# A sparse attention and mixer kernel: the identity made on GpSimd, and the first values and second pair's loads issued without a gate

## The chip, the core and the metric

The kernel runs on one core of a Trainium2 chip. Its time is the device time of one execution in microseconds; the times shown are of four runs, and the profile is of one more execution. The engines are TensorE (PE, with its weight loads as PEld), VectorE (DVE), ScalarE (ACT), GpSimd (POOL) and SyncE (SP), which issues most of the DMAs.

## The reference

The inputs are `q`, `k` and `v` of 4 batches x 8 heads x 768 positions x 64, three sampled blocks of keys for each of 24 blocks of 32 positions, and the weights of a mixer. The attention is masked by blocks: a block of queries sees its own block and its two neighbours, the first and the last block, and its sampled blocks; the first and last blocks of queries see all. The mixer mixes the positions by a low-rank product and then runs a two-layer network over the channels.

```python
scores = (q @ k.T) / sqrt(64);  scores = where(mask, scores, -1e9)
attn = softmax(scores);  x = attn @ v            # heads side by side: (4, 768, 512)
u = x + (x.transpose(0, 2, 1) @ U @ V).transpose(0, 2, 1)
out = u + relu(u @ w_ch1) @ w_ch2                # 512 -> 2048 -> 512
```

## The kernel before

The 32 heads are worked through in 16 pairs, numbered `i`; pairs 0 to 3 (`HP` = 4) make up the first batch. The loads of a pair's `q`, `k` and `v` are 384 KB each, in f32 (`src_of`, `new_ld`, `issue`, L220 to L234), into pools with two buffers of each kind. GpSimd casts them to f16 (`cast`, L236), TensorE transposes queries and keys in blocks of 128x128 by a matmul with an identity matrix `id16` (`turn_some`, L265; the transposed blocks are the tile `pturn`), and VectorE or ScalarE copies them from PSUM to `qa` and `ka` (`half_copy`, L417). The other half of the partitions of `qa` and `ka` holds the mask: `ka` one-hot rows of the key's block, which DMAs bring (`hot_rows`, L299), and `qa` a bias of 0 or -240 for each block of keys, made by a small matmul and a scaling (`mask_mm`, `mask_rows`, L375 to L398). One matmul so gives scores with their mask.

A pair has nine units `u`. For each one, TensorE writes 128x1024 scores (`psc`, L489), ScalarE takes the exponential (`est`, L498, always on ScalarE), and TensorE multiplies with the values three units later (`flush_value`, `pav`). At set units other work is put in by `at_unit` (L984): at unit 0 of pair 0 the second halves of the first queries and keys, the copies of the mask rows to the second set of `qa` (L999, by DMA on SyncE), the load of pair 2's queries and of the mixer's weights (L1003 to L1011), and the casts of pair 1 (L1012 to L1014); at units 4 and 6 the transposes of pair 1's queries and keys.

The order of work on each engine is the order of the program text (`keep`), so an engine that waits holds up all that is written behind it. After the first four pairs (from about 46 us) a planner in the kernel (`clk`, `later`, `try_unit`) lays out the remaining attention units between the matmuls of the mixer's network, in an order that is fixed when the kernel is built.

The start is written out by hand (L287 to L431). VectorE clears `zeros`, the mask halves and other tiles. GpSimd clears `Ut` and `Vt` and writes the column of ones in `vts`. SyncE issues the sampled blocks, the first pair's queries in two pieces (4 and 2 of 6 position groups), the second piece of its keys, and one-hot rows for one head; ScalarE issues a small table of constants, the first piece of the keys, the identity (L313) and one-hot rows for the other head, and then loads its table of exponentials with a dummy activation (L317). TensorE runs six warm-up matmuls on `zeros` (`warm_pe`). GpSimd casts the first piece of the keys, and VectorE that of the queries.

Behind these, the value load of pair 0 has a gate. GpSimd copies one column of the first keys' buffer `kld` into the value buffer `vld` (L335) once the first keys have landed and been cast. The load of `vld` on SyncE (L336) overwrites that column and so waits for the copy, and the three loads of pair 1 (`issue(1)`, L337) stand behind it on SyncE:

```python
vld = new_ld(0, "v")
keep(nc.gpsimd.tensor_copy(out=vld[:, 0, 0, 0:1], in_=kld[:, 0, 0, 0:1]))
keep(nc.sync.dma_start(out=vld, in_=src_of("v", 0)))
issue(1)
```

Of the kernel before, what the change touches and what calls it, by code (L numbers as in the profile page):

```python
# [15 lines left out]
ALU = mybir.AluOpType  # L16

P = 128
# [3 lines left out]
def kernel(  # L22
# [12 lines left out]
    nc = tc.nc  # L35
# [31 lines left out]
        [oh_np[:NB], ms_np, np.tile(np.arange(NB, dtype=np.float16), (NB, 1))], axis=1  # L67
    )
    small_np = np.concatenate([small_np, np.zeros_like(small_np[: 32 - NB])])
    eye16_np = np.eye(P, dtype=np.float16)  # L70

    small_dr = nc.inline_tensor(small_np, name="small_const")
    oh_dr = nc.inline_tensor(oh_np, name="onehot_const")
    eye16_dr = nc.inline_tensor(eye16_np, name="eye16_const")

    consts = ctx.enter_context(tc.tile_pool(name="consts", bufs=1))
    wpool = ctx.enter_context(tc.tile_pool(name="wpool", bufs=1))
# [21 lines left out]
    keep = tc.keep_in_program_order  # L99
# [95 lines left out]
    id16 = consts.tile([P, P], FP16)  # L195
# [7 lines left out]
    zeros = m01[:, T - 1, 0:P]  # L203
# [16 lines left out]
    def src_of(nm, i):  # L220
        b, hp = divmod(i, HP)
        return {"q": q, "k": k, "v": v}[nm][b, 2 * hp : 2 * hp + 2].rearrange(
            "h (p t) d -> p h t d", t=T
        )

    def new_ld(i, nm):
        lds[i, nm] = ldpool.tile([P, 2, T, D], FP32, tag="ld" + nm, name=nm + "ld")
        return lds[i, nm]

    def issue(i, names="qkv"):  # L230
        if i >= NPAIR:
            return
        for nm in names:
            keep(nc.sync.dma_start(out=new_ld(i, nm), in_=src_of(nm, i)))  # L234
# [55 lines left out]
    keep(nc.vector.memset(cbd, 0.0))  # L290
    for r in (slice(32, 64), rows[1]):
        keep(nc.vector.memset(small[r, 0:S], 0.0))
    keep(nc.gpsimd.memset(Ut, 0.0))
    keep(nc.gpsimd.memset(Vt, 0.0))
    qld, kld = new_ld(0, "q"), new_ld(0, "k")
# [3 lines left out]
    def hot_rows(eng, st, h, n):  # L299
# [5 lines left out]
            out=sbi[0:NB].rearrange("z r w -> z (r w)"),  # L305
            in_=sampled_blocks.bitcast(I32),
# [3 lines left out]
    keep(nc.scalar.dma_start(out=small[0:32], in_=small_dr.ap()))  # L310
    keep(nc.scalar.dma_start(out=kld[:, :, 0:TK], in_=k0[:, :, 0:TK]))
    keep(nc.sync.dma_start(out=qld[:, :, TQ:T], in_=q0[:, :, TQ:T]))
    keep(nc.scalar.dma_start(out=id16, in_=eye16_dr.ap()))  # L313
    keep(nc.sync.dma_start(out=kld[:, :, TK:T], in_=k0[:, :, TK:T]))
    hot_rows(nc.scalar, 0, 0, NB)
    hot_rows(nc.sync, 0, 1, NB)
# [6 lines left out]
    def cast0(eng, st, ld, t0, t1):  # L323
        keep(
            eng(
                out=st.rearrange("p t h d -> p h t d")[:, :, t0:t1],
                in_=ld[:, :, t0:t1],
            )
        )

    cast0(nc.gpsimd.tensor_copy, kst, kld, 0, TK)


    vld = new_ld(0, "v")
    keep(nc.gpsimd.tensor_copy(out=vld[:, 0, 0, 0:1], in_=kld[:, 0, 0, 0:1]))  # L335
    keep(nc.sync.dma_start(out=vld, in_=src_of("v", 0)))  # L336
    issue(1)  # L337

    warm = pst_tile([P, 512], FP32, "warm", tag="pav")
# [1 line left out]
    def warm_pe(n):  # L341
        for _ in range(n):
# [9 lines left out]
            out=eq[0:NB],  # L352
# [7 lines left out]
            out=cb[0:NB],  # L360
            in_=eq[0:NB].rearrange("z r c -> z c r"),
# [6 lines left out]
            out=cbd[0:NB, :, 0:NB],  # L368
# [697 lines left out]
    fill = deque()  # L1066
# [195 lines left out]
```

## Time and profile before

| What | Value |
|---|---|
| Four runs, median (lowest to highest) | 280.11 us (279.38 to 281.87) |
| The profiled execution | 279.39 us |
| Its span, from the first to the last instruction | 277.6 us |
| Busy: PE, PEld, DVE, ACT, POOL | 270.2, 161.5, 174.9, 177.2, 103.0 us |
| Granted TensorE clock | 1.0 of full speed |
| Mean DMA rate over the span | 114 GB/s |
| First exponential of ScalarE (L498) | 7.43 us |
| Exponentials of the first four pairs end | 45.71 us |
| First transposes (`pturn` from `qst`) | 5.60 us |
| Issue of the identity's DMA (L313), time to landing | 1.76 us, 3.8 us |

The times in the table's last four rows are from the start of the span. 1.8 us of the profiled execution lie outside its span. An idle time in a row stands before its instruction, and the name behind the arrow is what ended it. An engine's row with "xN" merges N instructions that follow one another. Rows marked SPq, ACTq or POOLq are an engine's DMA issues, which do not count as busy.

### The profile page before, as it was taken

Reading aid. Unit: us, or ns where it says so; the run is one execution under the profiler, and the core shown is the slowest. Engines: PE = TensorE matmul, PEld = TensorE weight load, DVE = VectorE, ACT = ScalarE, POOL = GpSimd, SP = SyncE. Lnnn points to the kernel's source line nnn. Section 1 sums busy time; section 2 is a strip of 40 time slices with the busy share of each in tenths; the row PEclk is TensorE's granted clock in tenths of the full one; section 3 lists DMA queues with packets and bytes.
Section 4 is the critical chain, followed back from the end, with each engine's and each line's share of the span. In section 5 each row is a group of like instructions: output and inputs, shape, how many; then the busy total and the mean of one; then the engine's idle time right before and its main releaser. Section 6 shows DMA issues by size and latency. Waiting matters only on the chain.

```text
span 277.6 us, 8037 instructions
## 1 busy us (share of the span) xinstructions
PE 270.2 (97%) x3492; PEld 161.5 (58%) x3492; DVE 174.9 (63%) x285; ACT 177.2 (64%) x198; POOL 103.0 (37%) x137
## 2 busy tenths in 40 slices
PE   7899999999999999999999999999999999999995
PEld 2568775566656564657565565656565655665443
DVE  6767767878887987777756768777777441000112
ACT  4989996787987857694855749584886201654000
POOL 4569549507374835363604536361102020000000
PEclk9999999999999999999999999999999999999999
DMA  5999975999969999996990999995100323000222
GB/s 140 292 302 302 269 181 84 190 180 82 144 46 94 190 124 140 158 99 78 69 104 0 181 93 169 133 95 77 31 2 2 104 79 94 12 1 0 78 76 77
DMA packets 85664, 31.72 MB, mean 114 GB/s; under 512 B 75308, under 2 KB 83228, under 8 KB 85628
## 3 DMA queue, kind: packets, MB, share of 16 engines
q0 software_dynamic: 49824, 10.29, 42.9%
q1 hardware_dynamic: 35304, 20.66, 35.0%
q8 instruction: 27, 0.44, 0.7%
q10 hardware_dynamic: 500, 0.25, 0.3%
q14 instruction: 9, 0.07, 0.1%
HBM read 27.91 MB, written 6.29 MB: 123 GB/s over the span
## 4 chain that ended last, share of the span: by engine, by line
PE 90%; DMA 4%; DVE 2%; POOL 1%; ACT 1%; issue 0%; ACTq 0%; SPq 0%; POOLq 0%; DVEq 0%
PE pch L175 30%; PE pt L175 30%; PE pav L175 13%; PE psc L175 12%; DMA qld<-in_q_dram 3%; PE pa L175 2%; DMA id<-eye_const 1%; PE ph L175 1%; PE pturn L268 1%; ACT est L498 1%; POOL xh L598 0%; PE puT L711 0%; DVE xh L541 0%; DVE xs L589 0%; PE pmk L175 0%
## 5 line engine op out<-in xcount | busy, mean ns | idle before, releaser
L498 ACT ACTIVATE est<-psc 128x1024 f16<-128x1024 f32 x144 | 143.2, 1028 | 45.5 <-PE psc L175 44.2
L175 PE MATMUL pt<-uT,w1t 64*128 64x384 f16 (+1 forms) x896 | 94.4, 324 | 0.0
L175 PE MATMUL pch<-w2t,tT 64*128 64x512 f16 (+3 forms) x688 | 93.6, 372 | 0.1
L519 DVE TENSOR_TENSOR est<-est,m 128x1024 f16<-128x1024 f16 x108 | 78.2, 739 | 18.2 <-ACT est L498 17.0
L175 PEld LDWEIGHTS <-w1t 64*128 64x128 f16 (+1 forms) x896 | 46.0, 95 | 36.2 <-PE pt L175 8.3
L175 PEld LDWEIGHTS <-tT 64*128 64x128 f16 (+1 forms) x688 | 38.2, 95 | 36.9 <-PE pch L175 1.6
L736 ACT ACTIVATE tT<-pt 128x768 f16<-128x768 f32 (+1 forms) x48 | 36.6, 772 | 26.0 <-PE pt L175 26.0
L175 PEld LDWEIGHTS <-est 128*128 128x128 f16 x1152 | 41.5, 97 | 10.9 <-issue 5.0
L175 PE MATMUL pav<-vt,est 128*128 128x65 f16 x1152 | 44.5, 193 | 0.2
L791 DVE TENSOR_TENSOR of<-xf,pch 128x1024 f32<-128x1024 f32 (+3 forms) x16 | 15.2, 950 | 42.7 <-PE pch L175 42.7
L175 PE MATMUL psc<-qT,kT 64*128 64x512 f16 (+1 forms) x288 | 40.6, 323 | 0.3 <-ACT est L498 0.3
L598 POOL CAST xh<-xs 128x768 f16<-128x768 f32 x12 | 10.5, 872 | 80.1 <-DVE xs L589 74.6
L684 POOL CAST uh<-xf 128x768 f16<-128x768 f32 x12 | 13.9, 1162 | 26.1 <-DVE xf L675 14.5
L738 DVE TENSOR_SCALAR tT<-pt 128x768 f16<-128x768 f32 (+1 forms) x20 | 18.3, 917 | 5.9 <-PE pt L175 5.8
L175 PE MATMUL psc<-qa,ka 128*128 128x512 f16 (+1 forms) x96 | 21.7, 326 | 0.2
L175 PEld LDWEIGHTS <-kT 64*128 64x128 f16 x288 | 14.6, 94 | 12.5 <-issue 0.7
L263 POOL DMA_DIRECT2D vt<-in_v_dram x20 | 16.3, 820 | 2.6 <-DMA w2t<-in_moe_w_ch_dram 2.6
L263 POOL DMA_DIRECT2D qst<-in_q_dram x20 | 16.3, 819 | 0.1
L263 POOL DMA_DIRECT2D kst<-in_k_dram x20 | 16.3, 820 | 0.0
L589 DVE TENSOR_TENSOR xs<-pav,rcp 128x768 f32<-128x768 f32 x12 | 11.5, 958 | 1.2
L675 DVE TENSOR_TENSOR xf<-xs,ph 128x768 f32<-128x768 f32 x12 | 11.4, 950 | 1.2 <-PE ph L175 1.2
L175 PEld LDWEIGHTS <-ka 128*128 128x128 f16 (+1 forms) x108 | 8.5, 97 | 3.5 <-issue 1.6
(69 smaller groups left out, 129.4 us busy)
## 6 DMA issues: line engine op xcount, KB each, us to landing
out_dram<-of SPq DMA_DIRECT2D x9, 512.0 KB, 3.3
vld<-in_v_dram SPq DMA_DIRECT2D x6, 384.0 KB, 7.0
w1t<-in_moe_w_ch_dram POOLq DMA_DIRECT2D x4, 512.0 KB, 8.7
w2t<-in_moe_w_ch_dram POOLq DMA_DIRECT2D x4, 512.0 KB, 9.8
qld<-in_q_dram SPq DMA_DIRECT2D x5, 384.0 KB, 6.2
kld<-in_k_dram SPq DMA_DIRECT2D x5, 384.0 KB, 6.7
qst<-in_q_dram POOLq DMA_DIRECT2D x20, 96.0 KB, 4.0
kst<-in_k_dram POOLq DMA_DIRECT2D x20, 96.0 KB, 4.5
```

Of the source, the lines that this page charges most:

```text
L175: ins = nc.tensor.matmul(out, lhsT, rhs, start=start, stop=stop, skip_group_check=loose)
L263: keep(nc.gpsimd.dma_start(out=o[:, h], in_=src_of(nm, i)[:, h]))
L268: nc.tensor.transpose(out=pt[:, t, :], in_=st[:, t].rearrange("p h d -> p (h d)"), identity=id16,)
L498: keep(nc.scalar.activation(out=est, in_=psc, func=AF.Exp, scale=0.125))
L519: keep(nc.vector.tensor_tensor(out=o, in0=o, in1=m, op=ALU.mult))
L589: nc.vector.tensor_tensor(out=xs.rearrange("p (c j) (h d) -> p c (j h) d", c=2, h=2), in0=pv[:, :, :, 0:D], in1=rcp[:, :, :, None].broadca ...
L598: keep(nc.gpsimd.tensor_copy(out=xh, in_=xs))
L675: nc.vector.tensor_tensor(out=u.rearrange("p (c j) n -> p c j n", c=2), in0=xs.rearrange("p (c j) n -> p c j n", c=2), in1=ph[:, :, 0:HS]. ...
L684: keep(nc.gpsimd.tensor_copy(out=uh, in_=u))
L736: keep(nc.scalar.activation(out=o, in_=i, func=AF.Relu))
L738: keep(nc.vector.tensor_scalar_max(out=o, in0=i, scalar1=0.0))
L791: nc.vector.tensor_add(out=of, in0=xfs[b][:, sc : sc + nsc, n0:n1], in1=pch)
```

## The change

The identity is no longer a constant in memory that a DMA on ScalarE's queue brings. GpSimd makes it in SBUF as its first work: an affine select reads `zeros` and writes 1 where the column's number equals the partition's, and the value read (0) elsewhere. GpSimd's column copy is gone, and the value load of pair 0 is issued by the same helper as the others, with nothing between it and SyncE's one-hot rows before it. The rest of the program, and the order on every engine, stays.

```diff
-    eye16_np = np.eye(P, dtype=np.float16)
...
-    eye16_dr = nc.inline_tensor(eye16_np, name="eye16_const")
...
     for r in (slice(32, 64), rows[1]):
         keep(nc.vector.memset(small[r, 0:S], 0.0))
+    keep(
+        nc.gpsimd.affine_select(
+            out=id16, in_=zeros, pattern=[[-1, P]], compare_op=ALU.not_equal,
+            fill=1.0, base=0, channel_multiplier=1,
+        )
+    )
     keep(nc.gpsimd.memset(Ut, 0.0))
...
     keep(nc.sync.dma_start(out=qld[:, :, TQ:T], in_=q0[:, :, TQ:T]))
-    keep(nc.scalar.dma_start(out=id16, in_=eye16_dr.ap()))
     keep(nc.sync.dma_start(out=kld[:, :, TK:T], in_=k0[:, :, TK:T]))
...
     cast0(nc.gpsimd.tensor_copy, kst, kld, 0, TK)
-
-
-    vld = new_ld(0, "v")
-    keep(nc.gpsimd.tensor_copy(out=vld[:, 0, 0, 0:1], in_=kld[:, 0, 0, 0:1]))
-    keep(nc.sync.dma_start(out=vld, in_=src_of("v", 0)))
+    issue(0, "v")
     issue(1)
```

## The prediction

> **What bounds the kernel now.** The page comes first, for the whole; then the busy time by stage, ScalarE's instructions in order of time, the chain of waits up to 25 us, and SyncE's issues. Busy time by stage (us, and instructions of each engine):
>
> ```profile
> 0.00:7.40 7.40, 5.50 (x20) 1.85 (x21) 4.71 (x15) 2.81 (x5) 3.80 (x13) 1.00 0.53 138
> 7.40:45.70 38.30, 36.43 (x521) 26.51 (x521) 27.65 (x61) 37.09 (x39) 25.37 (x39) 1.00 0.91 248
> 45.70:277.60 231.90, 228.24 (x2956) 133.14 (x2952) 142.50 (x211) 137.33 (x155) 73.87 (x87) 1.00 0.78 91
> ```
>
> The columns after the length are PE, PEld, DVE, ACT, POOL, then TensorE's granted clock (1.00), the DMA share and GB/s. From 45.7 us on TensorE is busy 228.24 of 231.90: that stage starts when the one before it ends, and a shift at its start goes through to the end. From 7.4 to 45.7 us ScalarE is the tightest engine, 37.09 of 38.30 us, and its gaps tell which wait ends last (the timeline of ScalarE; start, length, count, and the idle time before):
>
> ```profile
> 7.43 6.90 ACT L498 ACTIVATE est<-psc 128x1024 f16<-128x1024 f32 x7 [0.54 <-PE psc L175]
> 15.15 10.45 ACT L498 ACTIVATE est<-psc 128x1024 f16<-128x1024 f32 x11 [0.83 <-PE psc L175]
> ...
> 23.67 19.88 ACT L498 ACTIVATE est<-psc 128x1024 f16<-128x1024 f32 x21
> 43.77 1.94 ACT L498 ACTIVATE est<-psc 128x1024 f16<-128x1024 f32 x2 [0.22 <-PE psc L175]
> ```
>
> From the first exponential at 7.43 to 45.71 there are two gaps, 0.83 and 0.22 us. What lies behind the large one stands in TensorE's and GpSimd's timelines:
>
> ```profile
> 14.18 0.51 PE L268 MATMUL pturn<-id,kst 128*128 128x128 f16 x6 [0.89 <-POOL kst L249]
> ...
> 5.22 0.40 POOL L325 CAST kst<-kld 128x256 f16<-128x256 f32 x1 [2.61 <-DMA kld<-in_k_dram]
> 5.55 0.19 POOL L335 COPY vld<-kld 128x1 f32<-128x1 f32 x1
> 5.81 0.40 POOL L325 CAST qst<-qld 128x256 f16<-128x256 f32 x1
> 6.61 0.62 POOL L325 CAST kst<-kld 128x512 f16<-128x512 f32 x1 [0.40 <-DMA kld<-in_k_dram]
> ...
> 13.29 0.83 POOL L249 CAST kst<-kld 128x768 f16<-128x768 f32 x1 [2.55 <-DMA kld<-in_k_dram]
> ```
>
> The second pair's keys land at about 13.2 us; GpSimd casts them, TensorE (idle 0.89 us) turns them, and only then come scores for ScalarE. So the change matters in two places: the start of the first exponential, and this landing. The chain has the first:
>
> ```profile
> 1.76 3.80 DMA id<-eye_const
> 5.60 0.51 PE pturn L268 x6
> 6.11 0.40 DVE qa L417
> 6.54 0.44 DVE qa L417
> 7.02 0.39 PE psc L175
> 7.43 1.03 ACT est L498
> ```
>
> **Part 1: the identity's DMA goes.** Its landing is in the chain, so up to 5.60 − 5.36 us is offered: TensorE idled 0.78 us for it, while the queries it turns were cast by VectorE from 4.91 to 5.34. But what is late next is VectorE: after that cast it runs the mask rows (L387) from 5.37 for 0.69 us, to 6.06, and the copies of the turned queries start at 6.09. Queries turned by 5.36 + 0.4 instead of 6.0 wait there; the gain is 6.11 − 6.06, at most 0.05 us. ScalarE's key copies could start some 0.2 us earlier, but the scores also wait for VectorE's copies, to 6.97. ScalarE's queue loses a 0.49 us issue ahead of the exponential table's load; it then waits for TensorE at 4.45 to 4.86 anyhow. I take 0.
>
> **Part 2: the identity on GpSimd.** One affine select writes 128x128 f16, after a register move for its fill, ahead of the memsets (L293, L294, L319). It waits for VectorE's memset of `zeros` (0.82 + 0.11 = 0.93), where GpSimd now starts at 0.73: 0.2 us. The trace has no such operation. Below stands the 128x1 memset with 0.10 us, above the widest cast of this engine's early rows, 64x768 `Vt` with 1.57 us; nearest in reading, writing and elements is the 128x256 cast, 0.40 us, and I take that. All are hidden: GpSimd idles 2.61 us before its first key cast at 5.22, so 0.2 + 0.40 (even 0.2 + 1.57) end in that gap, and the identity is there by 2.6 us at the latest, before 5.34. Without the cover every us beyond 2.4 would move the key cast, and all behind it, by one. Queued behind the select are the memsets (consumers not before 8.9 us) and that cast. The removed copy of one column (L335, 0.19 us) gives nothing: the cast after it starts at 5.81 with its data landed at 5.76.
>
> The Trainium skill's GPSIMD Engine Reference, section Instruction dispatch, speaks against this part: the first call of a freshly loaded GpSimd kernel pays about 6 us of code loading that no row shows. If it held here, the identity would come near 7 us, the first key cast near 9, and the sum by it would be an estimated 282 us; no row of before shows whether it holds, since memsets, copies and casts all ran at once.
>
> **Part 3: the loads without the gate.** SyncE's issues now:
>
> ```profile
> 2.82 0.36 SPq L301 DMA_DIRECT2D ka<-onehot_const  x1
> 5.77 0.37 SPq L336 DMA_DIRECT2D vld<-in_v_dram  x1
> 6.19 0.47 SPq L234 DMA_DIRECT2D qld<-in_q_dram  x1
> 6.71 0.46 SPq L234 DMA_DIRECT2D kld<-in_k_dram  x1
> 7.21 0.47 SPq L234 DMA_DIRECT2D vld<-in_v_dram  x1
> 7.78 1.18 SPq L999 DMA_DIRECT2D qa<-qa  x2
> ```
>
> SyncE stands still from 3.18 to 5.77 behind the gate. "No gate" is not quite what results: the program's hardware-queue DMAs take eight completion counters in turn, and each waits for the one eight before it. With the identity's DMA gone the four loads wait for the small constants (2.7), the sampled blocks (2.5), the first queries (4.9) and the first keys (5.2). I expect issues near 3.2, 3.7, 4.9 and 5.4: 2.5, 2.5, 1.8 and 1.8 us earlier. What they gain in landing is less: in the trace SyncE's queue still carries the first keys and one-hot rows until about 6.1 us, and the values' first packets run at 6.75. The hole between, and the thin traffic before it (62 GB/s at 5.65, 0 from 6.15), is what fills: the stream moves up by 1.3 to 1.5 us. At the full rate of 64 packets of 1536 B per 0.25 us, 768 packets to the end of the second keys are 3 us, from about 5.3 to 8.4; before, the rate had halved from 9.25 us, with these keys in the middle. So they should land between 9.5 (no slowing) and 11.9 (13.24 − 1.35, the same slowing); I take 11. The gap closes from 13.24 − 0.89 = 12.35 on, so both ends close it: ScalarE goes from its 7th to its 8th exponential without the 0.83 us.
>
> What is late next: the second pair's scores (16.24 us, then 15.4) need its mask rows, copied by the L999 DMAs, landing at 15.55 and 15.86, and one-hot rows that GpSimd's queue lands at 14.2 and 14.8. The L999 copies wait for VectorE (7.3 and 7.76), so they issue only some 0.4 us earlier, but stand behind the four loads in the queue, which moves up 1.35: about 14.2 and 14.5, in time by 0.9 us. The third pair's queries (17.01, needed near 17.2 then) move up the same. Nothing after 45.7 us is timed by these loads.
>
> Against it stands a cost: from about 5.0 us the new packets share engines and memory with the tail of the first keys and the SyncE one-hot rows. In SyncE's queue they stand behind them, as the one-hot rows stand behind the keys (their 1536 B packets start at 5.25, with the keys nearly through). The tail's last landing is at 6.73, and the first scores need it by about 6.9. Packets of 1024 B took 42 ns there, those of 1536 B took 60 to 65 in the full stream; if the last 0.9 us of the tail stretches by a quarter to a half, it ends 0.2 to 0.4 us later, of which 0 to 0.2 us reaches the first exponential. I take 0.1.
>
> **The sum**, against the profiled execution: 0.05 (part 1, taken as 0) + 0 (part 2) − 0.83 + 0.1 = −0.73 us, so span 276.9 and execution 279.39 − 0.73 = 278.66. The four runs shown have the median 280.11, 0.72 above that execution; on them it is 279.4. Bounds: −0.83 − 0.05 − 0.22 (the later gap goes as well) = −1.1; for the other side, the rivals.
>
> **Rivals.**
> Given back (0.20): the gap moves from the 8th exponential to the 10th, since the mask rows hardly issue earlier. For it: 15.86 lies 0.4 us before use. Then 0.3 to 0.4 us are left: 279.8. Against: the queue ahead of them empties sooner.
> Crowded start, slower (0.15): the four loads share evenly with the tail of the first keys and one-hot rows. Place: first scores at 7.02. The 1.3 us from 4.9 to 6.2 double, so 1.3 − 0.2 of slack = 1.1 late, less 0.83: +0.3, 280.4; second key cast and GpSimd's one-hot rows (issued at 7.17) then slip as well, to +1.0, 281.1. It decides from a tail that lands after about 7.8. Against: the issue order in one queue.
> Not what it says (0.05): the counters' waits hold the loads near their old places, so nothing moves: 280.1.
> Slow select (0.05): past 2.4 us it shifts everything. At twice the upper row, 3.1 us, the loss of 0.7 meets the gain: 280.1; only far beyond that does it count.
>
> **How the numbers follow.** The forecast has 0.55 and gives 279.4. All cases lie within 1% (2.8 us), about what a measurement of this kernel can tell from no change, so 0.92 is for that; 0.05 for slower (a select or a crowded queue several us worse than any row), 0.03 for faster. The range goes from 280.11 − 1.1 to the crowded 281.1, with about 0.6 below for the spread of the runs (279.38 was the lowest of four).
>
> **What the changed profile would show.** A select on GpSimd near 0.95 us, shorter than 1.6; loads at 3.2, 3.7, 4.9, 5.4; no DMA hole at 6 us; the second key cast near 11 instead of 13.29; no 0.89 us wait of TensorE; 18 and more exponentials in one run from 7.45; the last of that stage ending near 45.0 instead of 45.71. The prediction is wrong if the first exponential starts after 7.7, or if a new gap opens at the second pair's first scores.

## The result and the profile after

The changed kernel takes 279.28 us (median of 54 runs, 278.26 to 280.81); the kernel before, measured beside it, 280.00 us (78 runs). The ratio is 0.9975, with a 95% interval from 0.9965 to 0.9984: 0.70 us faster, where 0.73 was forecast (279.4 us, range 278.4 to 281.1). It is within 1%, and the interval tells it from no change.

The profile, though, is of an execution of 280.81 us, the slowest of the 54. Its span is 279.0 us, 1.4 longer than the one before. It shows what goes wrong when this kernel's start goes wrong; profiles of faster executions stand below (e3, e11). First the granted clock over the span on the page (40 slices, tenths of full speed) and the busy time by stage, with the same columns as before:

```profile
PEclk9799999999999999999999999999999999999999
```

```profile
0.00:7.40 7.40, 5.12 (x18) 1.51 (x18) 4.79 (x15) 2.81 (x5) 3.45 (x12) 1.00 0.69 203
7.40:45.70 38.30, 37.28 (x512) 26.70 (x513) 26.22 (x57) 35.56 (x38) 24.99 (x39) 0.96 0.87 231
```

The DMAs' share in the first 7.4 us is 0.69 where it was 0.53, and 203 GB/s where it was 138: the hole is filled. But TensorE's granted clock averages only 0.96 of full speed in the second stage. ScalarE's timeline:

```profile
8.48 1.02 ACT L497 ACTIVATE est<-psc 128x1024 f16<-128x1024 f32 x1 [1.84 <-PE psc L173]
10.40 2.85 ACT L497 ACTIVATE est<-psc 128x1024 f16<-128x1024 f32 x3 [0.90 <-PE psc L173]
13.54 27.38 ACT L497 ACTIVATE est<-psc 128x1024 f16<-128x1024 f32 x29 [0.28 <-PE psc L173]
41.16 3.77 ACT L497 ACTIVATE est<-psc 128x1024 f16<-128x1024 f32 x4 [0.24 <-PE ph L173]
45.15 1.94 ACT L497 ACTIVATE est<-psc 128x1024 f16<-128x1024 f32 x2 [0.22 <-PE psc L173]
```

The gap before the 8th exponential is gone, since the run from 13.54 holds the 5th to the 33rd without one. In its place stand a first exponential at 8.48 instead of 7.43, gaps of 0.90 and 0.28 us behind it, and a new one of 0.24 us before the 34th. TensorE's timeline of the same execution names the first cause:

```profile
5.31 0.40 PE L266 MATMUL pturn<-id,qst 128*128 128x128 f16 x4 [0.60 <-DVE qst L328]
...
6.48 0.38 PE L173 MATMUL psc<-qa,ka 128*128 128x512 f16 x1
7.86 0.58 PE L173 MATMUL psc<-qa,ka 128*128 128x512 f16 x1 [1.00 <-DMA ka<-onehot_const]
8.24 0.63 PE L173 MATMUL warm<-m 128*128 128x512 f16 x1
```

The first transposes no longer wait for the identity but for the cast of the queries. Then the second half of the first scores waits 1.00 us for SyncE's one-hot rows, which landed at 7.72 instead of 6.73. From 7.88 to 11.29 us the clock's records are at half speed (in the rows: the single warm-up matmul takes 0.63 us instead of 0.38), and that makes the gaps of 0.90 and 0.28: e7 below has the same stretch and gaps of 0.90 and 0.31, while e6, nearly as late but at full clock, has 0.14 us before the second exponential and none before the 5th. SyncE's issues and GpSimd's timeline:

```profile
2.77 0.43 SPq L305 DMA_DIRECT2D ka<-onehot_const  x1
3.25 0.37 SPq L232 DMA_DIRECT2D vld<-in_v_dram  x1
3.66 0.47 SPq L232 DMA_DIRECT2D qld<-in_q_dram  x1
4.82 0.37 SPq L232 DMA_DIRECT2D kld<-in_k_dram  x1
5.23 0.47 SPq L232 DMA_DIRECT2D vld<-in_v_dram  x1
```

```profile
1.01 0.29 POOL L292 TENSOR_SCALAR_AFFINE_SELECT id<-m 128x128 f16<-128x128 f16 x1 [0.56 <-DVE m L285]
...
7.06 0.61 POOL L328 CAST kst<-kld 128x512 f16<-128x512 f32 x1 [1.19 <-DMA kld<-in_k_dram]
...
11.23 0.83 POOL L247 CAST kst<-kld 128x768 f16<-128x768 f32 x1 [0.63 <-DMA kld<-in_k_dram]
```

The select takes 0.29 us. The loads issue 2.5, 2.5, 1.9 and 2.0 us earlier, and the second pair's keys are cast at 11.23 instead of 13.29. But the second piece of the first keys is cast at 7.06 instead of 6.61: the tail is later, by 0.45 us.

### The profile page after: what moved, and what is told of

It reads as the page before. It is cut to its first block, busy times and chain, and to the rows that moved or that the text cites. A ratio compares the mean times of both kernels' runs of the same rounds, so it can differ in the third digit from the quotient of the medians.

```text
span 279.0 us, 8036 instructions
## 1 busy us (share of the span) xinstructions
PE 271.5 (97%) x3492; PEld 161.9 (58%) x3492; DVE 174.9 (63%) x285; ACT 177.1 (63%) x198; POOL 103.4 (37%) x137
## 4 chain that ended last, share of the span: by engine, by line
PE 92%; DVE 2%; ACT 2%; DMA 2%; issue 1%; POOL 0%; DVEq 0%; POOLq 0%
PE pch L173 30%; PE pt L173 30%; PE psc L173 14%; PE pav L173 13%; PE pa L173 2%; ACT est L497 2%; DMA ka<-onehot_const 2%; PE ph L173 1%; PE pturn L266 1%; PE pmk L173 1%; DVE m L459 1%; POOL xh L597 0%; PE puT L710 0%; DVE xh L540 0%; DVE xs L588 0%
## 5 line engine op out<-in xcount | busy, mean ns | idle before, releaser
L173 PE MATMUL psc<-qa,ka 128*128 128x512 f16 (+1 forms) x96 | 22.6, 339 | 1.4 <-DMA ka<-onehot_const 1.0
```

Source lines behind the costliest of these rows:

```text
L173: ins = nc.tensor.matmul(out, lhsT, rhs, start=start, stop=stop, skip_group_check=loose)
```

## The experiments

Two theories stood at the start. **A**: the earlier loads make the gain, by closing ScalarE's gap. **B**: the identity makes it, since its landing was in the chain. Differences of 0.3 us are 0.1%, less than most intervals here, so the verdicts rest on the traces as much as on the ratios. One measure helps: from the end of the 39th exponential, the last before the mixer takes over, to the end of the span, 12 of the 14 traces of this study take between 231.9 and 232.0 us. So all differences lie ahead of that, but for one in the two other traces (e1, e8).

### The ungated loads alone (e1, e8)

```diff
-    vld = new_ld(0, "v")
-    keep(nc.gpsimd.tensor_copy(out=vld[:, 0, 0, 0:1], in_=kld[:, 0, 0, 0:1]))
-    keep(nc.sync.dma_start(out=vld, in_=src_of("v", 0)))
+    issue(0, "v")
     issue(1)
```

> The identity still comes by its DMA; only the gate is gone. Theory A (the loads make the gain, by closing ScalarE's gap before its 8th exponential): ratio to the kernel before about 0.9975 as for the whole change, and no 0.8 us gap near 14 us. Theory B (the identity makes the gain, by taking its DMA out of the chain of the start): ratio 1.000 within 0.001. Both: the one-hot rows of SyncE's queue land at 6.7 to 7.7 us, and the first exponential starts between 7.4 and 8.4.

> The ungated loads alone once more, since their first ratio, 0.9987 with an interval from 0.9966 to 1.0009, tells neither theory from the other. Theory A: 0.9965 to 0.998, and the second pair's keys cast before 12.3 us with no gap before the 8th exponential. Theory B (the identity is needed for the gain): 0.999 to 1.000.

Measured: 279.89 us, ratio 0.9987 (0.9966 to 1.0009), and 280.00 us, 0.9999 (0.9986 to 1.0012). By the ratios A falls short. By the traces it holds: the keys are cast at 11.74 and 12.47, and neither has a gap before the 8th exponential. What eats the gain shows only in part. In the second trace the clock is granted only at 9.31 us, and the first exponential starts at 8.57. And both take 232.3 us behind the 39th exponential, 0.3 more than the others, of which the last experiments tell. The first trace has an early first exponential (7.23), but its execution, 279.21 us, is faster than its kernel's median, so it does not show what the typical one loses.

### The identity alone (e2)

This is the change without the lines of the experiment above.

> The identity is made on GpSimd; the gate and its column copy stay. Theory A: ratio 0.9995 to 1.000, since VectorE's mask rows hold the first copies to about 6.1 us whatever the identity does; first exponential at 7.4; the gap of about 0.8 us before the 8th exponential stays. Theory B: ratio 0.9975 and a first exponential before 7.2.

Measured: 280.16 us, ratio 0.9993 (0.9969 to 1.0016). ScalarE's timeline:

```profile
7.13 6.89 ACT L501 ACTIVATE est<-psc 128x1024 f16<-128x1024 f32 x7 [0.48 <-PE psc L173]
15.57 3.77 ACT L501 ACTIVATE est<-psc 128x1024 f16<-128x1024 f32 x4 [1.54 <-PE psc L173]
```

With the gate kept, the gap before the 8th exponential is there, and larger: 1.54 us, with the second pair's keys cast at 13.71. B gets no support. (The first exponential, at 7.13, did come before the 7.2 that B expected, but the cast of the queries started at 4.55 instead of 4.91, which the identity does not move.)

### The changed kernel again (e3, e11)

> The changed kernel as it stands, beside the others on one chip, with a second profile. Its first profile shows a start 1.05 us late (first exponential 8.48) and TensorE's clock halved from 7.9 to 11.3 us, in an execution of 280.81 us, the slowest of its 54. Theory A: that stall is of some executions only; ratio 0.9975, and a profile whose execution is near 279 shows the first exponential at 7.4 to 7.8 and a clock of 1.00 from 5 us on. If instead the late start is there in every execution, the second profile shows it too and the gain has another source than the closed gap.

> The changed kernel on the same chip as the three beside it, so that differences of 0.3 us can be read against it. Ratio 0.996 to 0.9975; the second pair's keys cast before 12.3 us, no gap before the 8th exponential, one of 0.2 us before the 34th.

Measured: 278.92 us, ratio 0.9961 (0.9939 to 0.9984), and 278.88 us, 0.9960 (0.9941 to 0.9979). ScalarE's timeline of the first of these, an execution of 278.61 us:

```profile
7.34 31.32 ACT L497 ACTIVATE est<-psc 128x1024 f16<-128x1024 f32 x33 [0.48 <-PE psc L173]
38.89 3.77 ACT L497 ACTIVATE est<-psc 128x1024 f16<-128x1024 f32 x4 [0.22 <-ACT est L497]
42.88 1.94 ACT L497 ACTIVATE est<-psc 128x1024 f16<-128x1024 f32 x2 [0.22 <-PE psc L173]
```

Here is the forecast picture: 33 exponentials in one run from 7.34 us, the keys cast at 10.32, the last exponential ending at 44.82 (45.0 was forecast). In the other trace the first exponential starts at 7.65, after a wait of 0.7 us for the one-hot rows. So the late start is a matter of degree, none, 0.7 or 1.0 us of waiting in three executions, and not a fixed cost.

### The start crowded, and uncrowded (e6, e4)

```diff
+    issue(0, "v")
     keep(nc.sync.dma_start(out=kld[:, :, TK:T], in_=k0[:, :, TK:T]))
...
-    issue(0, "v")
     issue(1)
```

> The changed kernel with the first values' load (384 KB) issued ahead of the second piece of the first keys and of SyncE's one-hot rows. It prices a crowded start: at some 330 GB/s these two land 1.2 us later than in the changed kernel (near 7.5 and 7.9 us). Theory A: the first exponential starts near 8.4, TensorE waits about 1 us for the one-hot rows in this profile as in the slow profile of the changed kernel, the gap before the 8th exponential stays closed, and the ratio is 1.000 to 1.003, that is 0.7 to 1.4 us slower than the changed kernel. Rival (the start has slack for the tail): as the changed kernel, 0.996 to 0.9975.

Measured: 279.89 us, ratio 1.0006 (0.9988 to 1.0025), against 0.9975 and 0.996 for the changed kernel. TensorE's timeline:

```profile
6.06 0.38 PE L173 MATMUL psc<-qa,ka 128*128 128x512 f16 x1
7.91 0.38 PE L173 MATMUL psc<-qa,ka 128*128 128x512 f16 x1 [1.47 <-DMA ka<-onehot_const]
```

A load of 384 KB put ahead of the tail costs a wait of 1.47 us for the one-hot rows and puts the first exponential at 8.32, with the gap before the 8th still closed. The whole gain is spent. The other way round, the one-hot rows go ahead of the second key piece:

```diff
+    hot_rows(nc.sync, 0, 1, NB)
     keep(nc.sync.dma_start(out=kld[:, :, TK:T], in_=k0[:, :, TK:T]))
     hot_rows(nc.scalar, 0, 0, NB)
-    hot_rows(nc.sync, 0, 1, NB)
```

> The changed kernel with SyncE's one-hot rows issued ahead of the second piece of the first keys, not behind it. Theory A with a crowded start (the new loads stretch the tail of SyncE's queue, and the first scores wait for its one-hot rows): these rows land before 6.5 us, TensorE's 1 us wait for them is gone, the first exponential starts at 7.4, and the ratio falls below that of the unchanged order by 0.0005 to 0.003, to 0.995 to 0.997. Rival (the tail is late in a rare execution only, and the median start is limited by VectorE): the same ratio as the unchanged order within 0.0007. Cost in both: the second piece of the keys lands some 0.1 us later.

Measured: 279.42 us, ratio 0.9973 (0.9950 to 0.9995), no better than the order of the change on the same chip (0.9961). TensorE's wait for the one-hot rows is gone and the first exponential starts at 7.08, earlier than the 7.4 expected. The second key piece, however, is cast only at 7.52, and TensorE's transposes wait for it:

```profile
8.19 0.40 PE L266 MATMUL pturn<-id,kst 128*128 128x128 f16 x4 [0.82 <-POOL kst L328]
```

TensorE waits 0.82 us for that instead, and ScalarE 0.96 us before its second exponential. I had put that cost at 0.1 us. Read with e6, the order of the tail's transfers only chooses who waits.

### The gate moved later (e5)

The gate's copy, the value load and `issue(1)` stand behind GpSimd's cast of the second key piece, and the copy reads that piece; the same four lines go from their old place (not shown).

```diff
     cast0(nc.gpsimd.tensor_copy, kst, kld, TK, T)
+    vld = new_ld(0, "v")
+    keep(nc.gpsimd.tensor_copy(out=vld[:, 0, 0, 0:1], in_=kld[:, 0, TK, 0:1]))
+    keep(nc.sync.dma_start(out=vld, in_=src_of("v", 0)))
+    issue(1)
```

> The kernel before, with its gate moved behind GpSimd's cast of the second piece of the first keys, so that the four loads issue near 7.4 us instead of 5.8. Theory A (the second pair's keys set ScalarE's gap before its 8th exponential): these keys are cast near 14.9 us, the gap grows from 0.8 to about 2.4 us, and the ratio is 1.004 to 1.006. Rival (the gap is a matter of the profiled execution, and the load has slack in most): ratio within 0.001 of 1.

Measured: 281.30 us, ratio 1.0039 (1.0013 to 1.0065). The loads issue 1.6 us later and cost 1.1 us: the median follows them in both directions. (Five of the 12 executions, though, took 279.6 to 280.2 us, as the kernel before does.) The place of the loss was not the one expected. TensorE's timeline:

```profile
11.86 0.42 PE L175 MATMUL pav<-vt,est 128*128 128x65 f16 x8 [1.85 <-POOL vt L243]
...
15.36 0.82 PE L268 MATMUL pturn<-id,qst 128*128 128x128 f16 x6 [1.24 <-POOL qst L249]
```

In this execution the first values come too late and then the second pair's queries, so the gap opens before the 5th exponential (2.63 us), ahead of the keys. Behind the first wait TensorE's clock is halved from 12.1 to 18.9 us; the execution took 283.77 us, the slowest of its kernel.

### The mask rows on ScalarE (e7)

```diff
-    mask_rows("dve", 0, pm0[:, 0, 0:QA], 0, QA)
     mask_rows("act", 1, pm1, 0, QA)
+    mask_rows("act", 0, pm0[:, 0, 0:QA], 0, QA)
```

> The changed kernel with VectorE's mask rows of head 0 moved to ScalarE. It tests the step that the identity gains nothing because VectorE's mask rows hold the first copies: if so, the copies now start about 0.3 us earlier with respect to the landing of the first queries, and the first exponential follows the cast of the first queries by some 2.2 us instead of 2.5; ratio 0.001 below the changed kernel, 0.9955 to 0.9965. Rival (TensorE's transposes or the one-hot rows hold the start): the distance stays at 2.5 us and the ratio at that of the changed kernel.

Measured: 279.08 us, ratio 0.9966 (0.9949 to 0.9984), as the changed kernel. VectorE's timeline of the changed kernel, and then of this one:

```profile
4.83 0.43 DVE L328 CAST qst<-qld 128x512 f16<-128x512 f32 x1 [1.10 <-DMA qld<-in_q_dram]
5.29 0.69 DVE L386 TENSOR_SCALAR qa<-pm 64x512 f16<-64x512 f32 x1
6.01 0.88 DVE L416 COPY qa<-pturn 64x512 f16<-64x512 f16 x2
```

```profile
4.50 0.43 DVE L328 CAST qst<-qld 128x512 f16<-128x512 f32 x1 [0.77 <-DMA qld<-in_q_dram]
5.43 0.88 DVE L416 COPY qa<-pturn 64x512 f16<-64x512 f16 x2 [0.50 <-PE pturn L266]
```

In the changed kernel the copies start 1.18 us behind the start of the cast, exactly as before (4.91 to 6.09): the mask rows did hold them, and against that trace the identity gained nothing. Without the mask rows it is 0.93 us, the 0.25 us offered.

Other traces with the identity's DMA show that this depends on the execution. In e1 the cast of the queries starts 0.43 us earlier than in the kernel before, the transposes, which wait for the identity, only 0.14 us (5.46, not 5.60), and the copies wait for them:

```profile
4.48 0.43 DVE L325 CAST qst<-qld 128x512 f16<-128x512 f32 x1 [0.74 <-DMA qld<-in_q_dram]
5.46 0.38 PE L268 MATMUL pturn<-id,qst 128*128 128x128 f16 x4 [0.67 <-DMA id<-eye_const]
5.88 0.87 DVE L415 COPY qa<-pturn 64x512 f16<-64x512 f16 x2 [0.25 <-PE pturn L268]
```

There, and in e5 (4.50 and 5.87), the copies start 1.40 and 1.37 us behind the cast's start (e8: 1.31; before and e10: 1.18). Every trace of an identity on GpSimd with the mask rows in place has 1.18 or 1.19. So with early queries the identity on GpSimd is worth some 0.2 us at the copies.

In e7 itself no time comes of the 0.25 us offered: in this execution the scores then waited 1.52 us for the one-hot rows, and the first exponential started at 9.01. What the median start gains is open.

### Two side effects of the number of instructions (e9, e10, e12)

The gap before the 34th exponential stood in every trace whose ScalarE had one instruction fewer than before, 335 rows in the trace (the change three times, e2, e4, e6), and in none with 336 (before, e1, e5, e7, e8). The 0.3 us at the end stood in the two traces whose GpSimd had the fewest, 202 rows (e1, e8), and in none with 203 or more. So each was given one harmless instruction in an idle place, to the changed kernel and to the identity alone on ScalarE, and to the ungated loads alone on GpSimd. The first added line below is that of e9 and e12, the second that of e10:

```diff
     keep(nc.scalar.activation(out=dummy, in_=zeros[:, 0:1], func=AF.Exp))
+    keep(nc.scalar.activation(out=dummy, in_=zeros[:, 0:1], func=AF.Exp))
...
+    keep(nc.gpsimd.memset(spare, 0.0))
     qst = stpool.tile([P, T, 2, D], FP16, tag="stq", name="qst")
```

> The changed kernel with one more activation of a single column on ScalarE right behind the first dummy one, where ScalarE idles. The traces of the kernels whose ScalarE has one instruction fewer than before (the identity's DMA) all show a gap of 0.22 to 0.24 us before its 34th exponential, and those with as many as before, or one moved there in its place, do not; TensorE then loses 0.3 us. If the place of the gap follows the number of ScalarE's instructions, it is gone here, the stage after the last of the 39 exponentials takes 232.0 us as always, and the ratio is 0.001 below the changed kernel's: 0.996. Rival (the gap comes from the identity on GpSimd itself): the gap stays and the ratio is that of the changed kernel.

Measured: 278.59 us (6 runs, 278.37 to 278.90), ratio 0.9939 (0.9920 to 0.9957), the fastest kernel of the study. The change on the same chip has 0.9960 (0.9941 to 0.9979), and the intervals overlap. ScalarE's timeline shows 37 exponentials in one run:

```profile
7.28 35.27 ACT L498 ACTIVATE est<-psc 128x1024 f16<-128x1024 f32 x37 [0.85 <-PE psc L173]
42.76 1.94 ACT L498 ACTIVATE est<-psc 128x1024 f16<-128x1024 f32 x2 [0.22 <-PE psc L173]
```

> The ungated loads alone, with one memset of a column more on GpSimd in an idle place. Both traces of the ungated loads alone show 0.3 us more between the last addition of the output and the end, in which two of GpSimd's semaphore instructions at the end take 0.38 us instead of 0.08. If that follows the number of GpSimd's instructions (one fewer there), it is gone: the stretch behind the last of the 39 exponentials falls from 232.27 to 231.95, and the ratio is 0.998 to 0.9985. If the identity still makes a difference beyond that, this kernel stays 0.3 us or more above the changed one; if not, the two are the same within 0.1 us, side effects set aside.

Measured: 278.83 us, ratio 0.9960 (0.9942 to 0.9978). The stretch behind the 39th exponential is 231.9 us again: the extra 0.3 is gone. And the ungated loads alone, with the identity still brought by its DMA, now stand where the changed kernel stands on the same chip (278.88 us, 0.9960). So the loads alone can make the whole gain, as A says. That they always do is not shown: the first two readings of the ungated loads are 1.1 us higher, and the end explains 0.3 of that. Beside the change on one chip, e1 is 0.97 us slower than e3 (279.89 and 278.92 us), though each carries one side effect of 0.3 us. With the side effects away on both sides, the change (e9) is 0.24 us faster than the loads alone (e10), and the intervals overlap. Whether the rest is scatter of the starts, or a share that the identity has beside the early loads, these runs do not settle.

> The identity on GpSimd with the gate kept, and one more one-column activation on ScalarE. If the identity gives nothing by itself and costs 0.3 us only by ScalarE's gap before the 34th exponential: no such gap, ratio 0.998 to 0.9995, the gap before the 8th exponential still there. If the identity has a gain of its own at the start (TensorE's wait for it falls from 0.78 to below 0.5 us): ratio 0.997 to 0.998, and no execution with a clock of 0.994, of which the kernel before has about one in ten.

Measured: 280.20 us, ratio 1.0009 (0.9989 to 1.0029). The gap before the 34th exponential is gone, the one before the 8th is 1.32 us, and two of 12 executions have a clock of 0.994 or less. With the gate kept the identity shows no gain, with or without the side effect; the intervals (0.9 us faster to 0.4 slower for e2, 0.3 faster to 0.8 slower here) do not exclude the 0.2 us seen at the copies in e1 and e5.

## Why the prediction was right, point by point

**Part 1, nothing gained from the identity's landing.** Right for the execution it was read from, and for the reason given: the copies stayed 1.18 us behind the cast's start, and e12 measures 1.0009. But "at most 0.05 us" was one execution's figure. In e1 and e5, with earlier queries, the wait for the identity put the copies some 0.2 us later, so the term is 0 to 0.2 us. e12 was also to tell whether the identity ends the executions at a clock of 0.994, and it has two at 0.994 or less.

**Part 2, the select at 0.40 us and hidden.** Right: 0.29 us, in the idle stretch. The rule weighed there, some 6 us of code loading on a first call (the Trainium skill, GPSIMD Engine Reference, section Instruction dispatch), does not show for this select: it started at 1.01 us, took 0.29, and nothing behind it was held up. (The 282 us named beside that rule is about 1 us low by part 2's own working: a first key cast at 9 instead of 5.22 moves all behind it by 3.8 us, from 279.4.) But the step that costed the removed issue on ScalarE at 0, in part 1, missed a term: with one instruction fewer there, a gap of 0.22 to 0.25 us opens before the 34th exponential. In the trace of e3 the lead over the kernel before falls there from 1.20 to 0.89 us. That is +0.3 us that the sum lacked.

**Part 3, the loads.** Right in its mechanism: issues forecast at 3.2, 3.7, 4.9 and 5.4 came at 3.25, 3.66, 4.82 and 5.23, keys forecast at 11 were cast at 10.32, 10.77 and 11.23, and the gap is closed in each of the ten traces with early loads. The second pair's mask rows were in time, so the rival "given back" did not come. The size of the term was off: 0.83 us was one execution's gap. The gated traces of before, e2 and e12 have 0.83, 1.54 and 1.32, so about 1.2 was on offer.

**The crowded start, taken at 0.1 us.** This term was sized too low. The tail was to end 0.2 to 0.4 us later. In the four traces with the gate (before, e2, e5, e12) SyncE's one-hot rows landed at 6.26 to 6.73 us, on average at 6.54; in the eight with the early loads behind them (the change three times, e1, e7 to e10) at 6.60 to 8.27, on average at 7.20: 0.7 us later. (The packets of 1024 B that entered the estimate took 46 ns in the trace, not 42.) For the first exponential: in the three traces of the change and in e9 the first exponential starts at 8.48, 7.34, 7.65 and 7.28, on average at 7.69; in before, e2 and e5 it starts at 7.43, 7.13 and 7.26, on average at 7.27 (e12, whose clock came only at 9.0 us, is left out; with its 8.16 the average is 7.50). That is 0.4 us, or 0.2 with e12, and in the slowest execution it costs more than the gap returns. The rival's place and price were right, as that execution (1.05 us) and e6 (0.89 us) show, and in one of three traces it decided. That the order in SyncE's queue holds it off in the others fits e6, where the load ahead of the tail costs more, but is not shown by itself. By the sign that the prediction set itself, a first exponential after 7.7 us, the first trace of the change (8.48) speaks against it and the two repeats (7.34, 7.65) do not; its other sign, a new gap at the second pair's first scores, came in none.

**The sum.** With the measured terms it is −1.2 + 0.4 + 0.3 = −0.5 us (−0.7 with e12 among the starts), by three to four executions a side. −0.70 was measured, and −1.1 in each of the two repeats. So the −0.73 is right in sign and place; that it met the first measurement within 0.03 us is luck, since its errors cancelled: a gain taken too small against two costs of which one was too small and one missing.

A part of the difference may lie in the clock; no run shows how much. Of the 98 executions of before in the three comparisons above, 7 have a mean clock of 0.994, and took 281.4 to 282.2 us; of the changed kernel's 78 one has (280.81). The half-speed stretch followed a long wait of TensorE in all three traces that have one (the change, e5, e7), but in e6 TensorE waited 1.47 us and kept the full clock. That the 0.89 us wait for the keys brings it on in the kernel before was not seen in a trace, and stays open.

## What to carry to other kernels

When a stage is bound by one engine, read its gaps one by one: the gap that is largest names the transfer that matters, and an early issue pays only as far as that transfer moves. Loads issued early can delay what is still in flight ahead of them (the one-hot rows here landed at 7.2 us on average instead of 6.5), so ask which landing the first work of the bottleneck needs and how much slack it has; here a tail of 0.3 us slack turned part of the gain into a late start. Size such terms from several executions, since the gap worth 0.83 us in one trace was 1.3 to 1.5 in others, and a wait that cost nothing in one cost 0.2 in two others. And where a change has two halves, measure each alone more than once: the loads alone gave 0.4, 0.0 and 1.1 us here, by the ratios.

## What was not expected of the hardware

One instruction more or fewer on an engine moved a stall. On ScalarE, removing a DMA issue at 1.8 us brought a gap of 0.22 to 0.25 us 37 to 39 us later, and a second dummy activation took it away. On GpSimd, removing a 0.19 us copy made two semaphore instructions at the very end start 0.38 us apart instead of 0.08, and one more memset undid it. What the stall is, no run here shows.

TensorE's clock was halved for a stretch of 3.41 us (the change, e7) or twice that (e5) within the first 20 us, when TensorE had waited 1.0 to 1.9 us, and not after the 1.47 us of e6; and the first grant came anywhere between 3.8 and 9.3 us though TensorE's first instructions are the same in all.
